# RetNet attention and a SwiGLU FFN on one core: the norm's sums by turned 32x32 blocks on VectorE, and the first turns of q on quarters of TensorE's array

## The chip, the cores and the metric

One core of a Trainium2 chip runs the kernel in one launch. The metric is the device time of an execution in microseconds (us), as the median of several runs. Engines are named as in the profile: PE (TensorE's products), PEld (its weight loads), DVE (VectorE), ACT (ScalarE), POOL (GpSimd), SP (SyncE, which issues most DMAs).

## What is computed

Attention without a softmax, with a decay for each head, and then a gated FFN with an RMS norm in front:

```python
# q, k, v: (8 batches, 8 heads, 576 positions, 64)
scores = scale * np.matmul(q, k.transpose(0, 1, 3, 2))
ret = scores * Dmat            # gamma_h ** (i - j) for i >= j, else 0
x = matmul(ret, v)             # heads side by side: 4608 tokens x 512
rms = np.sqrt(np.mean(x * x, axis=-1, keepdims=True) + 1e-06)
xn = x / rms * rms_g
g = xn @ w_gate                # 512 x 1536
out = (silu(g) * (xn @ w_val)) @ w_out   # 1536 x 512
```

w_gate, w_val and w_out come as float64 and are rounded to float32 on the chip.

## The kernel before, in words

**Attention.** A job is one batch and one pair of heads: 32 jobs, jobs 0 to 7 (batches 0 and 1) in a head of the program and the rest between the later FFN products. A job needs q and k with the head dimension on partitions. For jobs 0 to 7 `turn` makes them on PE with products by the identity: eight products for q (line 236, 64 of the array's columns each), four full transposes for k (line 230), and two transposes for the last 64 positions, the tail (line 245); ACT copies the results out of PSUM in four copies (lines 241 and 252). Later jobs are turned by DVE in `prepare`. `slot(j)` then does the values of job j-1 (`values`, line 379), the scores (line 292) and states (line 315) of job j on PE, the weighing of the scores (line 328) and the running sums of the states (line 341) on DVE, and the carried part of job j-1 (line 399). The scores and values are 64x64 products that use the four quarters of the array in turn; the carried ones of the first jobs use two. DVE writes the result into x (line 425).

**Units.** The 4608 tokens are nine units of 512. x of a unit is kept transposed, as 4 chunks of 128 channels x 512 tokens, so the norm's mean runs over partitions. Squares are ACT's (`square`), their sums over chunks DVE's (`gather`, lines 467 and 473).

**The norm.** For units 0 and 1, `norm_1` (line 481) takes the mean with eight products of one column, POOL raises it to -1/2, ACT writes it on the diagonal of four 128x128 blocks (`diagonals`, line 495), and a product of ones with these (line 546, called rb) broadcasts it to all partitions. For units 2 to 8, `root_1` sums over partitions and broadcasts at once with a product of ones with the squares, 128x512 (line 504), and finds the inverse root on full 128x512 tiles, by ACT (lines 506, 509, 516) and DVE (510, 513, 517), `root_2` going on with lines 526 and 529. `scale_x` (line 548) then scales x in four operations, and `sums_of_x` (line 563) forms the sums that the FFN's block products need.

**FFN.** Units 0 and 1 use `up_plain` (line 704, written U in the plan: U002 is unit 0, set 0, product 2) while the weights are still being rounded; units 2 to 8 use `up` (line 644), seven block products in each of six steps, and `across` (line 814) for the second matrix. The rounding of the weights runs in 36 halves, each of three ACT operations (line 1075), three DVE operations for the mantissa (1094, 1098, 1102) and a join (1119); a join lets its set's products start.

**Order.** All instructions are issued in program order on each engine, under a manual schedule. The first part is written out by hand in `PLAN`, one token a task: T turn, V scaling of v, S slot, C the close of the last job, Q a square, G a gather, N and D and X the norm's steps (R, Y and X for unit 2), w a step of the rounding, a an ACT step of it, A half a product of `across`. The later units run in a loop: in the last step of `up(u, 5)` the gathers and `root_1` of the next unit stand between its seven products, and `root_2`, `scale_x` and `sums_of_x` between those of `across(u)`. The loads are issued in the order of `LOADS`, the tails of q, k and v in `load_tails` (line 190), on ACT's queue for job 0 and on SP's for the others. PSUM has eight banks in one pool.

Of the kernel before, what the change touches and what calls it, by code (L numbers as in the profile page):

```python
# [14 lines left out]
P = 128  # L15
L = P // 2
SQ = 32
# [27 lines left out]
def kernel(  # L45
# [59 lines left out]
    mean_w = cell("mean_w", 1.0 / DM)  # L105
    mhalf = cell("mhalf", -0.5)
    eps = cell("eps", EPS)
    most = cell("most", 1151.0 + 7.5 / 16)
    top = cell("top", 255.0 * 2.0**23)
    guess = cell("guess", 0x5F1FFFF9 + 2.0**22 * np.log2(DM))  # L110
# [72 lines left out]
    def load_tails(i, queue):  # L183

        b, heads = TAILS[i]
        for n, (nm, src) in enumerate((("qt", q), ("kt", k), ("vt", v))):
            at = NV + (3 * b + n) * DM
            t = vi[:TAIL, at : at + DM].rearrange("p (h d) -> p h d", d=D)
            cut = slice(heads[0], heads[-1] + 1)
            queue.dma_start(  # L190
                out=t[:, cut], in_=src[b, cut, NFULL * P :].rearrange("h p d -> p h d")
            )
            for hp in range(heads[0] // 2, heads[-1] // 2 + 1):
                st[b * NHP + hp][nm] = t[:, 2 * hp : 2 * hp + 2]
# [27 lines left out]
    def turn(j):  # L222

        d = st[j]
        n = NFULL
        for nm in "qk":
            ps = bank(f"turn_{j}_{nm}")
            for c in range(n):
                if nm == "k":
                    nc.tensor.transpose(  # L230
                        out=ps[:, c * P : c * P + P],
                        in_=d["k"][:, c].rearrange("p e d -> p (e d)"), identity=ident,
                    )
                    continue
                for e in range(2):
                    nc.tensor.matmul(
                        ps[side(e), c : n * P : n], lhsT=d["q"][:, e, c], rhs=ident,
                        start=True, stop=True,
                    )
            t = d[nm + "T"] = att.tile([P, S], F32, tag=nm + "T", name=f"{nm}T_{j}")  # L240
            nc.scalar.copy(out=t[:, : n * P], in_=ps[:, : n * P])
        last = bank(f"turn_{j}_t")
        for i, nm in enumerate("qk"):
            o = slice(i * TAIL, i * TAIL + TAIL)
            nc.tensor.transpose(
                out=last[:, o], in_=d[nm + "t"].rearrange("p e d -> p (e d)"),
                identity=ident[:TAIL, :TAIL],
            )
        warm_up(j == 0, 2 * P)
        for i, nm in enumerate("qk"):  # L250
            o = slice(i * TAIL, i * TAIL + TAIL)
            nc.scalar.copy(out=d[nm + "T"][:, NFULL * P :], in_=last[:, o])
# [211 lines left out]
    def gather(u, c, sq):  # L464

        if c == NHP - 1 and u > 1:
            nc.vector.scalar_tensor_tensor(
                out=sq, in0=t_of[u], scalar=EPS * DM / P, in1=sq, op0=ALU.add, op1=ALU.add
            )
        elif u < 2 and c == NHP - 1:  # L470
            sq = (t_of[u], sq)
        elif c:
            nc.vector.tensor_tensor(out=sq, in0=t_of[u], in1=sq, op=ALU.add)
        t_of[u] = sq

    def norm_1(u):

        ms = bank(f"ms_{u}")
        for s in range(NS):
            for i, sq in enumerate(t_of[u]):  # L480
                nc.tensor.matmul(
                    ms[:, s : s + 1], lhsT=sq[:, s * P : s * P + P], rhs=mean_w,
                    start=(i == 0), stop=(i == 1),
                )
        r = tmp.tile([P, NS], F32, tag="r", name=f"r_{u}", bufs=1)
        nc.scalar.activation(out=r, in_=ms[:, :NS], func=AF.Relu, bias=eps)
        nc.gpsimd.tensor_tensor(out=r, in0=r, in1=mhalf.to_broadcast([P, NS]), op=ALU.pow)
        t_of[u] = r

    def diagonals(u):  # L490

        r = t_of[u]
        t_of[u] = row(f"diag_{u}")
        for s in range(NS):
            nc.scalar.activation(
                out=t_of[u][:, s * P : s * P + P], in_=ident, func=AF.Copy, scale=r[:, s : s + 1]
            )

    def root_1(u):


        y = t_of[u]
        s = bank(f"ms_{u}")
        nc.tensor.matmul(s, lhsT=ones, rhs=y, start=True, stop=True)
        e = row(f"e_{u}")
        nc.scalar.activation(
            out=y.bitcast(U32), in_=s.bitcast(U32), func=AF.Relu, bias=guess, scale=-0.5
        )
        nc.scalar.activation(out=e, in_=y, func=AF.Square)
        nc.vector.scalar_tensor_tensor(  # L510
            out=e, in0=e, scalar=-1.0 / DM, in1=s, op0=ALU.mult, op1=ALU.mult
        )
        nc.vector.scalar_tensor_tensor(
            out=y, in0=e, scalar=K0, in1=y, op0=ALU.add, op1=ALU.mult
        )
        nc.scalar.activation(out=e, in_=y, func=AF.Square)
        nc.vector.scalar_tensor_tensor(
            out=e, in0=e, scalar=K1 * K1 / DM, in1=s, op0=ALU.mult, op1=ALU.mult
        )
        t_of[u] = y, e  # L520

    def root_2(u):


        y, e = t_of[u]
        nc.vector.scalar_tensor_tensor(
            out=e, in0=e, scalar=-10.0 / 3.0, in1=e, op0=ALU.add, op1=ALU.mult
        )
        nc.vector.scalar_tensor_tensor(
            out=y, in0=e, scalar=5.0, in1=y, op0=ALU.add, op1=ALU.mult  # L530
        )
        t_of[u] = y
# [4 lines left out]
    def scale_x(u, chunks):  # L537
# [3 lines left out]
        g = rms_k  # L541
        rb = t_of[u]
        if u < 2:
            g = rms_g
            rb = bank(f"rb_{u}")
            nc.tensor.matmul(rb, lhsT=ones, rhs=t_of[u], start=True, stop=True)
        for c in chunks:
            nc.vector.scalar_tensor_tensor(
                out=x[:, c], in0=x[:, c], scalar=g[:, c : c + 1], in1=rb,
# [601 lines left out]
    def store_blocks(n):  # L1151
# [7 lines left out]
        T0 V0 a1 S0 a1 T1 a1 a1 V1 S1 T2 V2 F8 S2 V3 T3 w1 a1 w1 Q0 a1 a1 G0 Q1 a1 S3 T4 G1 V4  # L1159
        a1 a1 w1 Q2 a1 S4 a1 V5 w1 T5 G2 V6 Q3 a1 a1 G3 a1 S5 w1 T6 V7 w1 Q4 a1 S6 N0 a1 w1 a1  # L1160
        D0 a1 a1 G4 a1 T7 a1 w1 a1 w1 a1 a1 a1 Q5 X0 G5 S7 w1 U000 w1 a1 a1 a1 Q6 a1 C7 G6 a1 Q7
        G7 U001 N1 w1 w1 w1 D1 U002 w1 a1 X1 a1 w1 a1 w1 w1 w1 w1 a1 a1 a1 w1 a1 U003 a1 w1 w1
# [11 lines left out]
        G9 b1 i4 Q10 k0 Q11 a1 b2 A0 i5 A0 a1 a1 G10 A0 j6 A0 A0 A0 a1 P12 A0 j7 b3 A0 j8 c2 A1  # L1174
        c0 F13 A1 v1 A1 c3 A1 j9 o0 G11 A1 A1 j10 A1 A1 j11 A1 i12 A1 R2 A1 Y2 A1 X2 M2 p1 a1 a1
# [54 lines left out]
    def start():  # L1230
# [3 lines left out]
        def table(i, queue):  # L1234
# [25 lines left out]
            "G": lambda j: gather(*squares.pop(0)), "N": norm_1, "D": diagonals, "X": norm_2,  # L1260
# [6 lines left out]
            "r": refill, "W": weights_to, "A": lambda u: next(outs[u], None), "R": root_1,  # L1267
            "Y": root_2, "M": sums_of_x, "o": store, "p": lambda _: later.pop()(),
            "k": lambda _: nc.vector.tensor_scalar(
                out=rms_k, in0=rms_g, scalar1=3.0 / 8.0 * K1, scalar2=None, op0=ALU.mult  # L1270
            ), "U": lambda n: up_plain(n // 100, n // 10 % 10, n % 10),
# [8 lines left out]
    with tc.manual_schedule():  # L1280
        start()
        for u in range(2, NU):
            j0 = NHP * (u + 1)
            more = u + 1 < B
            for n in range(2 * NG):
                for i, _ in enumerate(up(u, n)):
# [9 lines left out]
                    if u + 1 < NU and n == 2 * NG - 1:  # L1296
                        if i < NHP:
                            gather(u + 1, i, square(u + 1, i))
                        elif i == NHP:
                            root_1(u + 1)  # L1300
# [7 lines left out]
            for i, _ in enumerate(across(u)):  # L1308
                if u + 1 == NU:
                    continue  # L1310
                if i == 2:
                    root_2(u + 1)
# [31 lines left out]
```

## Time and profile before

| | us |
|---|---|
| median of 3 runs | 1104.73 (1101.4 to 1110.42) |
| span of the profiled execution | 1104.5 |
| PE busy in the span | 1091.5 |
| DVE busy | 751.7 |
| ACT busy | 339.7 |
| POOL busy | 458.0 |
| first product of up for unit 0 (U000) | 57.38 |
| start of up for unit 2 | 306.02 |

The profile shows one execution of 1104.5 us; its own time is that of the middle run to 0.2 us. A line of a timeline gives the start, the time until the last instruction of the group ended, the engine, the line of the kernel, the operation, the tile written and those read, shapes and the number of instructions; in brackets stands how long the engine had nothing to do before, and what ended that. One float32 product is two instructions (passes) on PE, a float32 transpose one. Ends of PE's instructions are modelled and overlap, so PE's cost is read from start to start.

### The profile page before, as it was taken

The numbers are of one execution on the slowest core, as the hardware profiler recorded it, in microseconds if no ns is written. First come the engines' busy times: TensorE is split into PE (matmuls) and PEld (weight loads), VectorE is DVE, ScalarE is ACT, GpSimd is POOL, SyncE is SP. The second block draws the span as 40 slices with busy tenths as digits, with TensorE's granted clock in tenths as the row PEclk, the third lists the DMA queues.
The fourth block names the chain that finished last, engine by engine and source line by source line (L and its number), as shares of the span: only waits on it lengthen the run. The fifth ranks groups of instructions, "written<-read, shape, count | busy, mean of one in ns | idle before, by whom it ended". The sixth has DMA issues, their size and how long they took to land.

```text
span 1104.5 us, 24454 instructions
## 1 busy us (share of the span) xinstructions
PE 1091.5 (99%) x10102; PEld 915.1 (83%) x10102; DVE 751.7 (68%) x1219; ACT 339.7 (31%) x757; POOL 458.0 (41%) x421
## 2 busy tenths in 40 slices
PE   8899999999999999999999999999999999999998
PEld 7654444479988899889988998889888998898898
DVE  3778568877866794678657775668565935594457
ACT  5855564331124412342034303330233111211110
POOL 0026325538430196027802581239321942393236
PEclk9899999999999999999999999999999999999999
DMA  8847777696978866787678865887475755585461
GB/s 211 197 139 259 280 244 217 208 343 185 289 277 227 216 251 226 185 238 235 253 215 199 285 259 149 245 246 284 143 203 198 273 193 176 183 293 158 152 247 43
DMA packets 253871, 243.60 MB, mean 221 GB/s; under 512 B 193216, under 2 KB 213824, under 8 KB 247616
## 3 DMA queue, kind: packets, MB, share of 16 engines
q1 hardware_dynamic: 252320, 241.64, 69.1%
q8 instruction: 79, 1.29, 0.5%
q10 hardware_dynamic: 1440, 0.40, 0.2%
q14 instruction: 32, 0.26, 0.1%
HBM read 211.92 MB, written 30.08 MB: 219 GB/s over the span
## 4 chain that ended last, share of the span: by engine, by line
PE 96%; DVE 1%; issue 1%; ACT 0%; POOL 0%; POOLq 0%; DVEq 0%; ACTq 0%
PE up L704 15%; PE x L644 14%; PE w L644 13%; PE z L644 13%; PE y L644 7%; PE xo L814 6%; PE xp L814 4%; PE zo L814 4%; PE zp L814 3%; PE wo L814 2%; PE yo L814 2%; PE av L379 2%; PE wp L814 2%; PE av L399 2%; PE s L292 2%; PE yp L814 2%
## 5 line engine op out<-in xcount | busy, mean ns | idle before, releaser
L704 PE MATMUL up<-x,ring 128*128 128x512 f32 x384 | 167.1, 595 | 0.0
L644 PE MATMUL x<-x,ring 128*128 128x256 f32 x672 | 161.1, 383 | 0.0
L644 PE MATMUL w<-sums,ring 128*128 128x256 f32 x672 | 158.9, 379 | 0.0
L644 PE MATMUL z<-x,ring 128*128 128x256 f32 x672 | 158.8, 379 | 0.0
L766 POOL TENSOR_TENSOR vi<-h 128x384 f32<-128x384 f32 x32 | 39.5, 1234 | 275.2 <-DVE h L663 266.3
L704 PEld LDWEIGHTS up<-x,ring 128*128 128x128 f32 x384 | 72.3, 190 | 89.3 <-issue 84.8
L644 PEld LDWEIGHTS z<-x,ring 128*128 128x128 f32 x672 | 127.8, 190 | 19.8 <-issue 2.9
L644 PEld LDWEIGHTS w<-sums,ring 128*128 128x128 f32 x672 | 127.7, 190 | 17.2
L644 PEld LDWEIGHTS x<-x,ring 128*128 128x128 f32 x672 | 125.5, 190 | 17.4 <-ACT m L670 0.2
L771 POOL TENSOR_TENSOR vi<-h 128x384 f32<-128x384 f32 (+2 forms) x46 | 46.4, 1009 | 149.5 <-DVE h L663 149.5
L1010 POOL TENSOR_TENSOR vi<-vi 128x512 f32<-128x512 f32 (+1 forms) x77 | 78.1, 1027 | 37.9 <-DVE vi L841 21.5
L644 PE MATMUL y<-sums,ring 128*128 128x256 f32 x336 | 79.4, 379 | 0.0
L670 ACT COPY m<-x 128x512 f32<-128x512 f32 x42 | 24.6, 586 | 173.4 <-PE x L644 173.4
L651 DVE TENSOR_TENSOR h<-u,w 128x512 f32<-128x512 f32 x42 | 28.9, 688 | 67.8 <-PE w L644 67.8
L651 DVE TENSOR_TENSOR u<-m,y 128x512 f32<-128x512 f32 x42 | 28.8, 687 | 63.4 <-PE y L644 62.7
L644 PEld LDWEIGHTS y<-sums,ring 128*128 128x128 f32 x336 | 63.9, 190 | 8.6
L665 ACT ACTIVATE h<-h 128x512 f32<-128x512 f32 x63 | 39.7, 630 | 84.1 <-DVE h L651 84.1
L1130 POOL TENSOR_TENSOR vi<-vi 128x512 f32<-128x512 f32 (+1 forms) x24 | 40.7, 1696 | 30.8 <-DVE vi L1119 17.3
L651 DVE TENSOR_TENSOR u<-u,z 128x512 f32<-128x512 f32 x42 | 28.9, 688 | 33.7 <-PE z L644 33.6
L1130 POOL TENSOR_TENSOR ring<-ring 128x512 f32<-128x512 f32 x24 | 30.4, 1272 | 49.3 <-DMA w_up_blocks<-ring 44.1
L771 POOL TENSOR_TENSOR vi<-vi,h 128x384 f32<-128x384 f32 (+2 forms) x46 | 47.6, 1034 | 3.6
L771 POOL TENSOR_TENSOR vi<-h,vi 128x384 f32<-128x384 f32 (+2 forms) x46 | 46.9, 1019 | 3.6
(314 smaller groups left out, 2086.5 us busy)
## 6 DMA issues: line engine op xcount, KB each, us to landing
ring<-w_out_blocks SPq DMA_DIRECT2D x59, 1344.0 KB, 6.4
ring<-w_up_blocks SPq DMA_DIRECT2D x42, 1792.0 KB, 7.7
w_out_blocks<-vi SPq DMA_DIRECT2D x21, 448.0 KB, 5.9
out_dram<-vi SPq DMA_DIRECT2D x64, 128.0 KB, 3.0
qraw<-in_q_dram SPq DMA_DIRECT2D x96, 72.0 KB, 5.1
kraw<-in_k_dram SPq DMA_DIRECT2D x96, 72.0 KB, 2.5
k<-in_k_dram SPq DMA_DIRECT2D x48, 128.0 KB, 2.9
v<-in_v_dram SPq DMA_DIRECT2D x48, 128.0 KB, 2.8
```

The source lines that it names most:

```text
L292: nc.tensor.matmul(s[e][side(odd), i * L : i * L + L], lhsT=d["kT"][side(e), c * L : c * L + L], rhs=d["qT"][side(e), c * L : c * L + L], ...
L379: mm = nc.tensor.matmul(av[odd][column(j, odd, e), i * L : i * L + L], lhsT=d["v"][side(odd), i, e] if c < NC - 1 else d["vt"][:, e], rhs= ...
L644: nc.tensor.matmul(ps[:, i * HU : i * HU + HU], lhsT=w[:, PLACE[blk], c, i * P : i * P + P], rhs=t_of[u][blk][:, c], start=(start and i == ...
L651: nc.vector.tensor_tensor(out=o, in0=a, in1=pairs_of(ps), op=ALU.add)
L665: nc.scalar.activation(out=o, in_=c, func=AF.Silu)
L670: nc.scalar.copy(out=s1, in_=pairs_of(x_))
L704: nc.tensor.matmul(ps, lhsT=w[:, PLACE[blk], c % 2, i * P : i * P + P], rhs=x_of[u][:, c], start=(c == 0), stop=(c == NHP - 1),)
L766: eng.tensor_tensor(out=i1, in0=x12, in1=x11, op=ALU.subtract)
L771: eng.tensor_tensor(out=o[:, c], in0=a[:, c], in1=b[:, c], op=op)
L814: nc.tensor.matmul(ps, lhsT=lhs[:, c], rhs=w[:, s, c], start=((nm, s // 4) not in first), stop=False, skip_group_check=True,)
L1010: eng.tensor_tensor(out=t[:, :, o], in0=t[:, :, x], in1=t[:, :, y], op=ALU.add)
L1130: nc.gpsimd.tensor_tensor(out=t[o], in0=t[x], in1=t[y], op=op)
```

## The change

**The turn of jobs 0 to 7.** q is loaded as before, but each of its eight products is cut into two of 64x64, one for each half of the rows; the two halves write to two banks. The tails of q and k are loaded to the two halves of the partitions of one tile, and one full transpose turns both; it is issued ahead of k's four. ACT again makes four copies: q's first 256, its other 320, k's tail, k.

**The norm of all units.** The squares of all four chunks are summed (for units 0 and 1 two were summed and the rest left to the product). `fold` reduces the 128x512 sums over groups of 32 with a transpose inside 32x32 blocks, which gives 128x16; `meet` multiplies that with a 128x128 matrix `alike` that has ones where two partitions agree modulo 32; `root` finds the inverse root with eight DVE operations on 128x16, and a DVE transpose of the result, repeated along the free axis, writes it to all partitions of a PSUM bank as 128x512. `scale_x` reads that bank. `same_rows` makes `alike` from the identity in two DVE operations early in the plan. The factor rms_k, made late before, is now made ahead of X0.

**The plan.** For unit 0, N0 stands after G3 (before S5), R0 before S6, Y0 after it, k0 ahead of X0. For unit 1: N1 after G7, R1 after U001, Y1 two steps before U002. For unit 2: N2 two half products before R2. In the loop the fold takes the place of `root_1`, `meet` is issued after the seventh product, and `root` takes the place of `root_2`.

```diff
     def load_tails(i, queue):
         b, heads = TAILS[i]
-        for n, (nm, src) in enumerate((("qt", q), ("kt", k), ("vt", v))):
-            at = NV + (3 * b + n) * DM
-            t = vi[:TAIL, at : at + DM].rearrange("p (h d) -> p h d", d=D)
-            cut = slice(heads[0], heads[-1] + 1)
+        cut = slice(heads[0], heads[-1] + 1)
+        for n, (nm, src) in enumerate((("q", q), ("k", k), ("vt", v))):
+            at = NV + (2 * b + n // 2) * DM
+            t = vi[:, at : at + DM].rearrange("p (h d) -> p h d", d=D)
+            rows = side(n % 2)
...
     def turn(j):
-        for nm in "qk":
-            ps = bank(f"turn_{j}_{nm}")
...
-                for e in range(2):
-                    nc.tensor.matmul(
-                        ps[side(e), c : n * P : n], lhsT=d["q"][:, e, c], rhs=ident,
-                        start=True, stop=True,
-                    )
...
+        t = [bank(f"turn_{j}_q{r}") for r in range(2)]
+        for c in range(n):
+            for e in range(2):
+                for r in range(2):
+                    nc.tensor.matmul(
+                        t[r][side(e), c : n * L : n], lhsT=d["q"][side(r), e, c],
+                        rhs=ident[side(r), side(r)], start=True, stop=True,
                     )
+        m = n * L
+        nc.tensor.transpose(
+            out=t[1][:, m : m + P], in_=d["qkt"].rearrange("p e d -> p (e d)"), identity=ident
+        )
+        tk = bank(f"turn_{j}_k")
+        for c in range(n):
             nc.tensor.transpose(
-                out=last[:, o], in_=d[nm + "t"].rearrange("p e d -> p (e d)"),
-                identity=ident[:TAIL, :TAIL],
+                out=tk[:, c * P : c * P + P], in_=d["k"][:, c].rearrange("p e d -> p (e d)"),
+                identity=ident,
             )
...
+        nc.scalar.copy(out=qT[:, :m], in_=t[0][:, :m])
+        nc.scalar.copy(out=qT[:, m:], in_=t[1][:, : m + TAIL])
+        nc.scalar.copy(out=kT[:, n * P :], in_=t[1][:, m + TAIL : m + 2 * TAIL])
+        nc.scalar.copy(out=kT[:, : n * P], in_=tk)
...
     def gather(u, c, sq):
-        if c == NHP - 1 and u > 1:
+        if c == NHP - 1:
...
-        elif u < 2 and c == NHP - 1:
-            sq = (t_of[u], sq)
...
-    def norm_1(u):
...
-    def diagonals(u):
...
-    def root_1(u):
...
-    def root_2(u):
...
+    def fold(u):
+        t = column_of(f"fold_{u}")
+        nc.vector.tensor_reduce(
+            out=t, in_=t_of[u].rearrange("p (b j) -> p b j", j=SQ), axis=mybir.AxisListType.X,
+            op=ALU.add, apply_transpose=True,
+        )
+        t_of[u] = t
...
+    def meet(u):
+        t = t_of[u]
+        s = t_of[u] = bank(f"ms_{u}")[:, :NB]
+        nc.tensor.matmul(s, lhsT=alike, rhs=t, start=True, stop=True)
...
+    def root(u):
+        s = t_of[u]
+        y, e = column_of(f"y_{u}"), column_of(f"e_{u}")
+        def step(o, a, c, b, op0, op1=ALU.mult):
+            nc.vector.scalar_tensor_tensor(out=o, in0=a, scalar=c, in1=b, op0=op0, op1=op1)
+        nc.vector.tensor_scalar(
+            out=y.bitcast(U32), in0=s.bitcast(U32), scalar1=-0.5, scalar2=GUESS,
+            op0=ALU.mult, op1=ALU.add,
         )
+        nc.vector.tensor_tensor(out=e, in0=y, in1=y, op=ALU.mult)
+        step(e, e, -1.0 / DM, s, ALU.mult)
+        step(y, e, K0, y, ALU.add)
+        nc.vector.tensor_tensor(out=e, in0=y, in1=y, op=ALU.mult)
+        step(e, e, K1 * K1 / DM, s, ALU.mult)
+        step(e, e, -10.0 / 3.0, e, ALU.add)
+        step(y, e, 5.0, y, ALU.add)
+        t_of[u] = bank(f"rows_{u}")
+        nc.vector.transpose(
+            out=t_of[u].rearrange("p (b j) -> p b j", j=SQ),
+            in_=y.unsqueeze(2).to_broadcast([P, NB, SQ]),
+        )
...
     def scale_x(u, chunks):
...
-        if u < 2:
-            g = rms_g
-            rb = bank(f"rb_{u}")
-            nc.tensor.matmul(rb, lhsT=ones, rhs=t_of[u], start=True, stop=True)
...
     PLAN = """
-        T0 V0 a1 S0 a1 T1 a1 a1 V1 S1 T2 V2 F8 S2 V3 T3 w1 a1 w1 Q0 a1 a1 G0 Q1 a1 S3 T4 G1 V4
-        a1 a1 w1 Q2 a1 S4 a1 V5 w1 T5 G2 V6 Q3 a1 a1 G3 a1 S5 w1 T6 V7 w1 Q4 a1 S6 N0 a1 w1 a1
-        D0 a1 a1 G4 a1 T7 a1 w1 a1 w1 a1 a1 a1 Q5 X0 G5 S7 w1 U000 w1 a1 a1 a1 Q6 a1 C7 G6 a1 Q7
-        G7 U001 N1 w1 w1 w1 D1 U002 w1 a1 X1 a1 w1 a1 w1 w1 w1 w1 a1 a1 a1 w1 a1 U003 a1 w1 w1
+        T0 V0 a1 S0 K0 a1 T1 a1 a1 V1 S1 T2 V2 F8 S2 V3 T3 w1 a1 w1 Q0 a1 a1 G0 Q1 a1 S3 T4 G1 V4
+        a1 a1 w1 Q2 a1 S4 a1 V5 w1 T5 G2 V6 Q3 a1 a1 G3 N0 a1 S5 w1 T6 V7 w1 Q4 a1 R0 S6 Y0 a1 w1 a1
+        a1 a1 G4 a1 T7 a1 w1 a1 w1 a1 a1 a1 Q5 k0 X0 G5 S7 w1 U000 w1 a1 a1 a1 Q6 a1 C7 G6 a1 Q7
+        G7 N1 U001 R1 w1 w1 Y1 w1 U002 w1 a1 X1 a1 w1 a1 w1 w1 w1 w1 a1 a1 a1 w1 a1 U003 a1 w1 w1
...
                         elif i == NHP:
-                            root_1(u + 1)
+                            fold(u + 1)
+                        elif i == 6:
+                            meet(u + 1)
...
                 if i == 2:
-                    root_2(u + 1)
+                    root(u + 1)
```

## The prediction

> **What bounds the kernel now.** I read the page first, then the busy time by stage, then the timelines of the two places that the change touches. The page's first part puts TensorE (PE) at 99% of the span. The busy time by stage says where that figure can be trusted (columns: stretch, its length, then busy time with instructions of PE, PEld, DVE, ACT, POOL; granted clock; DMA share; GB/s).
>
> ```profile
> PE 1091.5 (99%) x10102; PEld 915.1 (83%) x10102; DVE 751.7 (68%) x1219; ACT 339.7 (31%) x757; POOL 458.0 (41%) x421
> ```
>
> ```profile
> 29.68:50.90 21.22, 18.49 (x515) 16.04 (x513) 19.94 (x53) 16.96 (x45) 1.29 (x4) 0.96 0.88 212
> 50.90:73.00 22.10, 21.83 (x257) 12.96 (x256) 13.09 (x30) 10.23 (x22) 4.18 (x6) 0.89 0.44 123
> 73.00:306.00 233.00, 232.27 (x1510) 143.60 (x1510) 178.45 (x300) 97.65 (x191) 114.77 (x95) 1.00 0.76 251
> 306.00:1093.00 787.00, 786.14 (x7161) 714.76 (x7160) 522.25 (x778) 197.42 (x455) 333.58 (x301) 1.00 0.68 217
> ```
>
> There are two regimes. From 73 us on PE is busy for 1018.4 of 1020 us at clock 1.00: what leaves its queue there leaves the span. In the head it isn't so: from 29.68 to 50.90 VectorE (DVE) is busy for 19.94 of 21.22 us and PE for 18.49. The head holds all eight turns and the norms of units 0 and 1; the steady part holds seven norms.
>
> One norm of the steady part on PE:
>
> ```profile
> 503.79 1.02 PE L504 MATMUL ms<-sq,ones 128*128 128x512 f32 x2
> 504.64 1.89 PE L644 MATMUL z<-x,ring 128*128 128x256 f32 x8
> ```
>
> PE loses 504.64 - 503.79 = 0.85 us to it, with no wait ahead. In the head, first PE, then DVE:
>
> ```profile
> 8.25 0.81 PE L292 MATMUL s<-qT,kT 64*64 64x64 f32 x40
> 8.88 0.28 PE L315 MATMUL s<-h 64*64 64x64 f32 x2
> ...
> 23.27 1.09 PE L236 MATMUL turn_q<-ident,h 128*64 128x128 f32 x16
> 24.30 0.65 PE L230 MATMUL turn_k<-ident,h 128*128 128x128 f32 x4
> 24.89 0.34 PE L245 MATMUL turn_t<-ident,vi 64*128 64x64 f32 x2
> ...
> 45.37 1.95 PE L481 MATMUL ms<-mean_w,sq 128*128 128x1 f32 x16
> 47.24 0.87 PE L236 MATMUL turn_q<-ident,ring 128*64 128x128 f32 x11
> 49.43 0.80 PE L236 MATMUL turn_q<-ident,ring 128*64 128x128 f32 x5 [1.32 <-issue]
> ...
> 51.61 2.08 PE L546 MATMUL rb<-diag,ones 128*128 128x512 f32 x2
> ...
> 57.38 3.70 PE L704 MATMUL up<-x,ring 128*128 128x512 f32 x8
> ```
>
> ```profile
> 29.68 0.48 DVE L341 SCALAR_TENSOR_TENSOR sum<-sum,gc,last 128x256 f32<-128x256 f32 x1 [2.19 <-ACT sum L349]
> ...
> 53.72 2.72 DVE L548 SCALAR_TENSOR_TENSOR x<-x,rms_g,rb 128x512 f32<-128x512 f32 x4 [2.83 <-PE rb L546]
> ...
> 63.28 0.95 DVE L425 TENSOR_TENSOR x<-av,gq 128x256 f32<-128x256 f32 x4 [2.29 <-PE av L399]
> ...
> 72.98 2.72 DVE L548 SCALAR_TENSOR_TENSOR x<-x,rms_g,rb 128x512 f32<-128x512 f32 x4 [3.65 <-PE rb L546]
> ```
>
> The reader is to see DVE's idle brackets: between 29.68 and the scaling of unit 0 it really waits once, 2.83 us for the broadcast rb, and that wait is what the change removes while it puts work of its own in the same place.
>
> **The change, part by part: the seven norms of units 2 to 8.** PE drops the 128x512 product with ones, 0.85 us, and gets meet, two passes of 16 columns. Small full-array products cost (47.24 - 45.37)/16 = 0.117 us a pass in the row of L481, so meet is 0.23 us. From below, two passes at the 0.016 us of the score row are 0.03; from above, half the wide product, 0.43. I take 0.23, the nearest in shape: 7 x 0.62 = **4.3 us off the path**, ends 2.9 and 5.7. Does meet wait? It needs fold, and fold's DVE queue is free at 505.49, after the multiplication into h that begins at 504.71 and takes 0.78. PE reaches meet after products z and w, moved up to 503.79 (1.73 each, from 504.64 to the next row's 506.37): 507.25. Fold has 1.76 us; the dense 128x512 row of DVE is 0.69. For unit 2 fold stands behind work that ends at 290.80 and meet comes at 293.11. No wait. Behind meet, PE's next unit needs x; today the sums of x end at 532.3 and PE wants them at 540.9, so 8.6 us cover root. There DVE drops five wide operations (0.69 + 1.17 + 0.69 + 1.21 + 1.37 = 5.1 us) for fold, eight narrow ones and a transpose, 3.3 us by the rows below. ScalarE's three operations a norm and GpSimd's power go too; PE waits for neither, so nothing is counted.
>
> **The head, DVE.** New in unit 0 ahead of the scaling: the third sum (0.69), a wait for ScalarE's square 3 (it ends at 39.69, DVE is free at about 39.1: 0.6), fold (0.69), root, and 0.2 for rms_k. Root is eight dependent 128x16 operations and a transpose. The row of dependent 128x64 operations of L341 has 285 ns, its 128x192 ones 413, so 1.0 ns an element: 285 - 48 = 0.24 us each, 1.9 in all; bounds 1.3 (the 128x64 product of L425, 216 ns, less 48) and 2.5 (0.31 start to start). [...] The transpose: 736 to 771 ns for 576 elements, 0.70 for 512. So root 2.6, and all of it 4.8 us. DVE ended its queue at 50.89, so X0 starts at 50.89 + 4.8 = 55.7, against 53.72. What PE does earlier doesn't move this: DVE is full from 29.68, and that start hangs on ScalarE, busy without a gap from 24.47, after only 0.34 us of idle time. same_rows lies in DVE's 2.6 us of idle time before 14.90.
>
> **The head, PE.** A turn's q: 16 passes in 24.30 - 23.27 = 1.03 us become 32 on quarters in the order of the scores, whose row has 40 in 8.88 - 8.25 = 0.63 us: 0.50. Tails: two products, 25.15 (the next row) - 24.89 = 0.26 us, become one like a quarter of k's 0.59: 0.15. That is 0.64 us a turn, 5.1 for eight; the norms of 0 and 1 free 1.87 + 2.0 + 1.70 + 0.86 - 2 x 0.23 = 6.0. All 11 us are PE time, and DVE takes the cover away. Both tail loads keep their number, queue and place, but the tail product now stands ahead of k's: job 1's tail came at 13.26, so k's 0.59 and its copy start behind that wait, some 0.85 us later, which the faster turns of jobs 2 and 3 pay back. The four ScalarE copies of a turn stay four, 0.1 us longer. For the PSUM bank that rows_0 holds from Y0 to X0 I count nothing: if turn 7 had to wait for one, PE stands there anyway, and the price is nothing until the 6 us below are used up.
>
> PE comes to U000 some 6 us early and stands until x's first chunk, 55.7 + 0.74 = 56.4, against 57.38. A standing PE has a price here:
>
> ```profile
> 48.00:49.00 1.00, 0.11 (x3) 0.00 (x0) 0.99 (x4) 0.97 (x3) 0.72 (x1) 1.00 0.54 82
> 49.00:50.00 1.00, 0.57 (x5) 0.40 (x4) 0.96 (x2) 1.00 (x4) 0.00 (x0) 0.57 0.55 90
> 50.00:51.00 1.00, 1.00 (x7) 0.71 (x4) 0.85 (x2) 0.73 (x2) 0.00 (x0) 0.50 0.82 134
> ```
>
> After 1.4 us of standing the granted clock is 0.50 until 56, and rb takes 2.0 us for 0.86. The same over U000 would add 0 to 3.5 us to its 3.6. [...] From U000's end (60.0 to 63.5; today 61.0) values and carried of job 7 follow (2.1), then on DVE x (0.95), two sums (1.3), fold (0.7), and the three mantissa operations and the join that U002 needs (2.5): 62.1 + 5.5 = 67.6 or, late, 71. DVE's own sum says no earlier than 68.5: X0's end 58.4, then 0.6 + 0.8 + 1.7 + 0.9 + 0.6 of job 7's work, 63.0, and the same 5.5. U002 started at 68.40 today and U003 at 72.78; now U002 starts at 68.5 to 71 and U003 3.5 later, 72.0 to 74.5. X1 (root and one step later, 73 to 75) meets U100 in time. That is a gain of 0.8 or a loss of 1.7, by the clock; **I take 0**. The ends add root's bounds, 0.6 us in each of two units: a gain of 2.0 and a loss of 2.9.
>
> **Sum.** The profiled execution spans 1104.5, 0.2 below the median 1104.73, so what lies around it is 0.2. 1104.5 - 4.3 - 0 + 0.2 = **1100.4**, 0.4% less; with the ends, 1104.7 - 5.7 - 2.0 = 1097.0 to 1104.7 - 2.9 + 2.9 = 1104.7.
>
> **Rivals.** (1) The head pays in full: DVE isn't what holds U000, or its new operations are short. Against it: 19.94 busy of 21.22. For it: PE is itself at 18.49 and much waits crosswise. 1104.7 - 4.3 - 11.0 = 1089.4; half of it, 1095. (2) Slower: no row shows a reduction with a transpose. If it ran at a quarter of the dense rate, fold is 2.8 us: each head norm loses 2.1 and each of units 3 to 8 has PE waiting 1.0 at meet, 4.2 + 6.0 - 4.3 = 5.9, so 1110.6; at an eighth (5.5 us), 1132. It decides from fold = 2.05 us (2 x 1.36 + 6 x 0.29 = 4.4). For it: the shape is new; against it: the 32x32 transposes run at the dense rate. (3) The quarters do not overlap, as in the row of L399 (32 passes in about 1.05 us): the turns gain nothing, but the head is DVE's; 1100.4 again, at most 1101.
>
> **How the numbers follow.** The forecast with (3) has 0.77, (1) 0.13, (2) 0.10. About 1% (11 us) is what a measurement of this kernel can tell from no change: its runs lie from 1101.4 to 1110.4. Faster by more needs less than 1093.7: nearly all of (1), 0.12. Slower by more needs over 1115.8: fold beyond 3.4 us, 0.05. Within: 0.83. The range takes the forecast's ends and the half of (1), 1095, on one side, the near half of (2) on the other: 1094 to 1107.
>
> **What would show it.** Right: meet without idle time before it, about 0.25 us between its neighbours' starts; fold near 0.7 us; idle PE before U000 with DVE as releaser and a clock under 1.00; X0 near 55.7; U003 within 2 us of 72.8. Wrong: U000 before 54 (the head pays), or PE waiting on fold at meet (the slower case).

## The result, and the profile after

The changed kernel takes 1112.72 us (median of 9 runs, 1109.64 to 1116.55), the kernel before 1105.25 beside it (9 runs, 1101.4 to 1110.42): ratio 1.0063, 95% interval 1.0048 to 1.0079. It is 7 us slower, where 4.3 us less were forecast. The profiled execution took 1113.29, with a span of 1111.5 for 1104.5.

The page's first part, and the busy time by stage over the same stretches as before (columns as there):

```profile
PE 1080.1 (97%) x10190; PEld 908.2 (82%) x10190; DVE 737.5 (66%) x1275; ACT 322.9 (29%) x726; POOL 441.4 (40%) x419
```

```profile
29.68:50.90 21.22, 14.12 (x561) 12.98 (x562) 16.30 (x42) 14.58 (x40) 0.27 (x3) 0.96 0.82 205
50.90:73.00 22.10, 19.38 (x299) 12.03 (x297) 19.69 (x54) 10.04 (x19) 1.55 (x4) 0.88 0.43 112
73.00:306.00 233.00, 224.68 (x1414) 133.76 (x1415) 176.88 (x296) 96.87 (x189) 112.16 (x92) 0.99 0.75 237
306.00:1093.00 787.00, 786.50 (x7198) 717.93 (x7198) 499.61 (x817) 185.85 (x437) 317.08 (x299) 1.00 0.71 222
```

Every engine has less to do, and the span is longer. PE's busy time fell by 11.4 us. The prediction had reckoned with 15.4 (4.3 and 11); on the pages the up products of the FFN alone take 4.0 us of it back (171.1 us in all for 167.1), since some of them ran at a lower clock (0.50 from 59.60 to 62.90, U000 below among them, and from 80.10 to 86.80). The gaps between PE's instructions grew by 18 us. The last row is as full as before, so the loss is ahead of it. The first row holds what the forecast ruled out: DVE, full there before with 19.94 us, has 16.30, and PE 14.12. Both wait.

The steady part did what it should. PE around meet, in the norm of the same unit as before, and the fold ahead of it on DVE:

```profile
514.79 1.89 PE L637 MATMUL w<-sums,ring 128*128 128x256 f32 x8
516.51 0.29 PE L505 MATMUL ms<-fold,alike 128*128 128x16 f32 x2
516.65 1.58 PE L807 MATMUL xo<-ring,h 128*128 128x128 f32 x12
```

```profile
514.68 0.70 DVE L483 TRANSPOSE_TENSOR_REDUCE fold<-sq 128x16 f32<-128x512 f32 x1
```

From meet's start to its neighbour's it is 0.14 us for 0.85, with no wait. From the start of up for unit 2 to the end, 798.48 us became 794.29 (1104.5 - 306.02 and 1111.5 - 317.21): 4.2 less for six norms. That start itself moved from 306.02 to 317.21, and there the loss is. PE at the end of the head:

```profile
49.33 0.69 PE L295 MATMUL s<-qT,kT 64*64 64x64 f32 x14 [3.46 <-issue]
...
58.67 0.33 PE L402 MATMUL av<-qT,sum 64*64 64x64 f32 x3 [1.40 <-issue]
...
59.68 5.29 PE L697 MATMUL up<-x,ring 128*128 128x512 f32 x8 [0.68 <-DVE x L541]
...
67.05 3.70 PE L697 MATMUL up<-x,ring 128*128 128x512 f32 x8
...
72.87 1.98 PE L697 MATMUL up<-x,ring 128*128 128x512 f32 x4 [0.18 <-DVE ring L1112]
82.45 27.75 PE L697 MATMUL up<-x,ring 128*128 128x512 f32 x59 [7.59 <-DVE x L541]
```

U000 starts at 59.68 (57.38 before), and its eight passes take 5.29 us for 3.70. The row at 82.45 begins with U003, which stands 7.59 us and is released by L541, the scaling. U003 belongs to unit 0, whose x has been ready since 61.5. The DVE rows beside it:

```profile
58.78 2.72 DVE L541 SCALAR_TENSOR_TENSOR x<-x,rms_k,rows 128x512 f32<-128x512 f32 x4
...
72.74 0.17 DVE L515 TENSOR_SCALAR y<-ms 128x16 uint32<-128x16 uint32 x1
72.94 1.25 DVE L519 TENSOR_TENSOR e<-y 128x16 f32<-128x16 f32 x1
74.23 0.17 DVE L513 SCALAR_TENSOR_TENSOR e<-e,ms 128x16 f32<-128x16 f32 x1
74.43 1.10 DVE L513 SCALAR_TENSOR_TENSOR y<-e,y 128x16 f32<-128x16 f32 x1
...
79.68 2.71 DVE L541 SCALAR_TENSOR_TENSOR x<-x,rms_k,rows 128x512 f32<-128x512 f32 x4
```

X0 is at 58.78, X1 at 79.68 (53.72 and 72.98 before). X1's last reading of rows_1 ends at 82.39, and U003 starts 0.06 us later: it has waited for a unit that it doesn't read.

Last, PE's waits from 0 to 90 us that the profile puts down to "issue" (PE stood idle, and waited for nothing that the profile shows): before, then after (columns: what waited, for what, us in all, times, longest). An idle time of PE is called a stand below.

```profile
PE turn_q L236 <- issue: 2.3, 2, 1.3
...
PE av L399 <- issue: 0.8, 1, 0.8
...
PE s L292 <- issue: 0.4, 1, 0.4
```

```profile
PE av L402 <- issue: 4.3, 3, 1.8
PE s L295 <- issue: 3.5, 1, 3.5
...
PE s L318 <- issue: 1.5, 1, 1.5
PE turn_q L235 <- issue: 1.3, 1, 1.3
...
PE av L382 <- issue: 0.7, 1, 0.7
```

3.5 us became 11.3. (The texts below count 4.8 and 12.2: the same sums over the whole span.)

### The profile page after: what moved, and what is told of

Read it like the earlier page. It is cut to its first block, busy times and chain, and to the rows that moved or that the text cites. A ratio compares the mean times of both kernels' runs of the same rounds, so it can differ in the third digit from the quotient of the medians.

```text
span 1111.5 us, 24657 instructions
## 1 busy us (share of the span) xinstructions
PE 1080.1 (97%) x10190; PEld 908.2 (82%) x10190; DVE 737.5 (66%) x1275; ACT 322.9 (29%) x726; POOL 441.4 (40%) x419
## 4 chain that ended last, share of the span: by engine, by line
PE 94%; DVE 3%; issue 1%; DMA 1%; SPq 0%; ACT 0%; POOL 0%; POOLq 0%; DVEq 0%; ACTq 0%
PE up L697 15%; PE x L637 13%; PE w L637 13%; PE z L637 13%; PE y L637 7%; PE xo L807 6%; PE xp L807 4%; PE zo L807 4%; PE zp L807 3%; PE wo L807 2%; PE yo L807 2%; PE av L382 2%; PE s L295 2%; PE wp L807 2%; PE av L402 2%; PE yp L807 2%
## 5 line engine op out<-in xcount | busy, mean ns | idle before, releaser
L697 PE MATMUL up<-x,ring 128*128 128x512 f32 x384 | 171.1, 605 | 8.4 <-DVE x L541 8.3
L759 POOL TENSOR_TENSOR vi<-h 128x384 f32<-128x384 f32 x32 | 42.8, 1338 | 274.5 <-DVE h L656 264.8
L764 POOL TENSOR_TENSOR vi<-h 128x384 f32<-128x384 f32 (+2 forms) x46 | 43.8, 953 | 150.2 <-DVE h L656 150.2
L426 ACT COPY x<-av 128x192 f32<-128x192 f32 (+6 forms) x136 | 37.8, 278 | 29.5 <-PE av L402 28.0
L764 POOL TENSOR_TENSOR vi<-h,vi 128x384 f32<-128x384 f32 (+2 forms) x46 | 44.6, 969 | 3.6
```

The lines of the kernel that those rows point to most:

```text
L426: nc.scalar.copy(out=o, in_=part)
L697: nc.tensor.matmul(ps, lhsT=w[:, PLACE[blk], c % 2, i * P : i * P + P], rhs=x_of[u][:, c], start=(c == 0), stop=(c == NHP - 1),)
L759: eng.tensor_tensor(out=i1, in0=x12, in1=x11, op=ALU.subtract)
L764: eng.tensor_tensor(out=o[:, c], in0=a[:, c], in1=b[:, c], op=op)
```

## The experiments

Four theories. **1, the bank:** the eight PSUM banks are handed out in turn, and rows_1, which lies in one from root to the end of the scaling, holds U003's. **2, the quarters:** the turn in twice as many PE instructions makes PE stand for issue. **3, the tail** ahead of k's four products holds the turns of the first jobs. **4, VectorE's work:** the head's norms put fold and root on a DVE that is already full. All ratios are to the kernel before on the same chip, with 95% intervals; a difference of two ratios is turned into us with 1105.5.

### The parts by themselves

**Rows in SBUF.** In the changed kernel:

```diff
-        t_of[u] = bank(f"rows_{u}")
+        t_of[u] = temp(f"rows_{u}") if u < 2 else bank(f"rows_{u}")
```

> The changed kernel, but for units 0 and 1 root writes its row of factors into SBUF and not into a PSUM bank. Theory 1 (bank): the eight banks go round in order, and the eighth request after rows_1 is the bank of U003, so U003 stands 7.59 us until X1 has read rows_1 for the last time (82.39; U003 at 82.45). Without it U003 follows U002 at about 74.9, U100 is then held by X1's first chunk (about 80.4), and of the 7.6 us and the half clock behind them (5.3 us for eight passes in place of 3.6) some 6 to 8 come back: 1105 to 1107. Theory 2 (the quarters: PE's idle time put down to issue, 12.2 us in the changed kernel's head against 4.8): the same lateness shows up at the next product, and no more than 2 us come back: 1111 to 1113. Theory 3 (the tail product ahead of k's four): no change, 1112 to 1113.

Measured: 1108.15 us, ratio 1.0029 (1.0015 to 1.0043), 3.8 us less than the changed kernel's ratio gives. PE from U002's second half on:

```profile
76.12 1.98 PE L697 MATMUL up<-x,ring 128*128 128x512 f32 x4 [0.18 <-DVE ring L1112]
78.80 3.70 PE L697 MATMUL up<-x,ring 128*128 128x512 f32 x8 [0.69 <-ACT h L705]
83.82 3.67 PE L697 MATMUL up<-x,ring 128*128 128x512 f32 x8 [1.33 <-DVE x L541]
89.06 6.25 PE L697 MATMUL up<-x,ring 128*128 128x512 f32 x14 [1.56 <-DVE ring L1112]
```

U003 (78.80) follows U002 and no longer waits for X1; 7.59 us of standing became 0.69 + 1.33 + 1.56 = 3.58. The profile names no banks: that U003 lay in that of rows_1 is shown by its wait for X1's last reading and by this test. Less came back than the 6 to 8 us expected, since U100 (83.82) and U110 (89.06) now stand for X1 and for their weights. The edit moves unit 0's row too, so what came back is the price of both rows.

**The norm alone**, with the old turn and loads:

```diff
-        t = [bank(f"turn_{j}_q{r}") for r in range(2)]
...
+        for nm in "qk":
+            ps = bank(f"turn_{j}_{nm}")
```

> The changed kernel with the old turn and the old loads of tails: the new norm alone. It asks for as many PSUM banks in the same order, so theory 1 (bank) keeps U003 behind X1: 1109 to 1113, with U003 at the end of X1. Theory 2 (the quarters) says that the head's loss goes away with the turn, and the steady part's 4.9 us stay: 1100 to 1104, idle time by issue back near 5 us. Theory 3 (tail product first) says 1 to 3 us less than the changed kernel: 1110 to 1112.

Measured: 1110.45, ratio 1.0048 (1.0032 to 1.0064), issue back at 4.3 us, and U003 again stands 7.59 us for X1. As theory 1 said; theory 2 alone is out.

**The turn alone**, on the kernel before:

```diff
-        for nm in "qk":
-            ps = bank(f"turn_{j}_{nm}")
...
+        t = [bank(f"turn_{j}_q{r}") for r in range(2)]
```

> The kernel before with the turn on quarters and the new loads of tails, and the old norm. Theory 1 (bank): no row of factors is held in PSUM from root to scaling, so the head loses nothing by it; VectorE bounds the head and the turn gains nothing: 1103 to 1106. Theory 2 (the quarters): it loses most of the changed kernel's 11.2 us in the head: 1110 to 1116, with some 12 us of idle time by issue. Theory 3: 1106 to 1108.

Measured: 1111.81, ratio 1.0062 (1.0045 to 1.0079). So theory 1 alone is out too: the turn by itself loses 6.9 us, and U003 doesn't stand in it. Its waits for issue, from 0 to 90 us, sum to 9.6:

```profile
PE s L295 <- issue: 3.1, 1, 3.1
PE turn_q L235 <- issue: 2.1, 1, 2.1
PE s L318 <- issue: 1.8, 1, 1.8
PE av L402 <- issue: 1.8, 1, 1.8
...
PE av L382 <- issue: 0.8, 1, 0.8
```

After the longest, 3.08 us up to 49.55, the clock is at half (0.50 from 50 to 60). Busy time and clock of that stretch (the eighth column is the clock; before: 0.66):

```profile
48.00:58.00 10.00, 8.45 (x130) 8.21 (x131) 4.01 (x12) 2.08 (x6) 1.02 (x1) 0.54 0.77 153
```

**The steady part alone:** the new norm in units 2 to 8 only, on the kernel before.

```diff
+            "n": fold, "R": meet, "Y": root, "K": same_rows,
...
-                            root_1(u + 1)
+                            fold(u + 1)
```

> The kernel before with the new norm in units 2 to 8 alone; units 0 and 1, the turn and the tails as before. All theories put the loss into the head, so here the steady part's 4.9 us stand by themselves: 1100 to 1101, a ratio of 0.9955 to the kernel before. If it comes out above 1103, the loss isn't in the head.

Measured: 1101.34 (1098.42 to 1102.64), ratio 0.9960 (0.9945 to 0.9974): 4.4 us less. This is the fastest version measured, and the forecast's one real gain by itself.

### What issue is

The trace's DMA records have a queue of kind instruction (q8 on the page), with 79 packets of 16 KB before and 80 after. 10102 passes of PE and as many weight loads in 79 packets make 256 PE instructions each. In each of the 17 traces of this study the number of packets is that of PE's instructions divided by 256 and rounded up (78 to 81). In these traces there are 63 stands for issue longer than 0.6 us in the first 90 us, and every one ends 2.2 to 3.3 us after such a packet's transfer began. In the dense stretch of the changed kernel the packets begin 4.1 to 4.5 us apart (18.3, 22.8, 27.0, 31.5, 35.9, 40.0). So PE, as far as can be inferred, has run out of program. The longest of these stands takes 4.0 us (e_pad2 below). The agreement of stands and packets is no proof that the count of instructions decides the time, so it was varied.

**Padding the old turn**, 256 PE instructions more in the head:

```diff
+        for e in range(8):
+            nc.tensor.matmul(
+                last[side(e % 2), 2 * TAIL : 2 * TAIL + 1], lhsT=d["k"][side(e % 2), 0, 0],
+                rhs=d["k"][side(e % 2), 0, 0, :1], start=True, stop=True,
+            )
```

> The kernel before, with the old turn and eight idle quarter products of one column behind the tails of each turn (16 passes with their weight loads, some 0.26 us a turn, no result used): as many PE instructions as the turn on quarters has, 256 more in the head. Theory 2 in its sharper form (PE's instructions come in 16 KB pieces of 256, each about 2.2 to 3.0 us after its request, and every idle time put down to issue ends so): 2 to 6 us more than the kernel before, 1107 to 1111, and idle time by issue over 7 us. Rival (the quarters themselves disturb the array, or the copies of a turn in their new order): 1104.5 to 1107.

Measured: 1109.89, ratio 1.0030 (1.0017 to 1.0043), 3.3 us more; issue 6.1 us, less than the 7 expected. But the idle products take longer than the 0.26 us a turn that was reckoned: in job 2 they begin at 18.49 and the values behind them at 18.87, so 0.38 us, or 3.0 us for eight turns. Their own time can make up the whole loss, and this run doesn't decide for theory 2.

**Twice the padding:**

```diff
-        for e in range(8):
+        for e in range(16):
```

> As e_pad with sixteen idle quarter products behind the tails of each turn: 512 PE instructions more in the head than before, two pieces of 16 KB. Theory 2 (instructions): twice e_pad's loss of 3.3 us or more, 1111 to 1115. Rival (e_pad's loss was a shift of where the pieces fall): 1106 to 1110.

Measured: 1117.82, ratio 1.0122 (1.0090 to 1.0155): 13.5 us more, four times the loss for twice the padding. The sixteen products of a turn take 0.84 us from their start to that of the values behind them, 6.7 us for eight turns:

```profile
36.83 1.03 PE L250 MATMUL turn_t<-ring 64*64 64x1 f32 x29
37.67 0.27 PE L384 MATMUL av<-ret,h 64*64 64x64 f32 x1
```

So some 7 us are left. Issue sums to 6.9 us, 3.4 more than before, and one stand alone is 4.0:

```profile
PE av L404 <- issue: 4.4, 2, 4.0
PE turn_q L236 <- issue: 2.5, 2, 1.5
```

Here the padding costs more than its own time, but what the rest consists of wasn't separated. Padding adds work as well as instructions; the next run takes instructions away and leaves PE's time nearly as it is.

**The other direction:** the turn on quarters with 256 instructions taken away (it adds 240). Half of carried's products of the first eight jobs (the second head) are left out, and that part of x is not computed.

```diff
-            for e in range(2):
+            for e in range(1 if j < FIRST else 2):
                 mm = nc.tensor.matmul(
                     av[odd][column(j, odd, e), i * L : i * L + L], lhsT=d["sum"][side(e), c - 1],
```

> The turn on quarters alone, and in the first eight jobs the products of carried for the second head left out: eight products, 16 passes and 16 weight loads a job, so that the head has as many PE instructions as before the change. (That part of x is then not computed.) Theory 2 (instructions): idle time by issue back to 5 us or less, and most of the turn's loss gone: 1104 to 1107. Rival (the quarters or the order of the copies cost, whatever the count of instructions): some 2 us less for the shorter carried, 1109 to 1111.

Measured: 1105.39, ratio 1.0004 (0.9986 to 1.0023). 6.4 us of the turn's 6.9 are gone, and issue falls from 9.6 to 5.9:

```profile
PE turn_q L235 <- issue: 2.8, 2, 1.8
...
PE av L402 <- issue: 1.1, 1, 1.1
PE last L318 <- issue: 0.8, 1, 0.8
...
PE av L382 <- issue: 0.6, 1, 0.6
PE s L295 <- issue: 0.6, 1, 0.6
```

PE's work hardly got shorter: from the start of carried to that of the turn's tail product (line 240) PE takes 1.54 us in the turn alone and 1.49 with half of carried's products left out. In the turn alone, then here:

```profile
42.76 1.08 PE L402 MATMUL av<-qT,sum 64*64 64x64 f32 x30
...
44.30 0.33 PE L240 MATMUL turn_q<-ident,vi 128*128 128x128 f32 x1
```

```profile
35.24 1.03 PE L402 MATMUL av<-qT,sum 64*64 64x64 f32 x15
...
36.73 0.33 PE L240 MATMUL turn_q<-ident,vi 128*128 128x128 f32 x1
```

This is the test that decides for theory 2: fewer instructions for nearly the same work, and the loss is gone.

**Its control**, the same products left out of the kernel before (that part of x is not computed there either):

```diff
-            for e in range(2):
+            for e in range(1 if j < FIRST else 2):
```

> The control of e_less_turn: the kernel before with the same products of carried left out (that part of x is not computed), 256 instructions fewer in the head than it had. Theory 2 (instructions): idle time by issue under 3.5 us, 1 to 4 us less than the kernel before: 1102 to 1105. Rival: less by the shorter carried alone, at most 2 us, 1104 to 1106; then e_less_turn stands 5 us or more above it.

Measured: 1106.51, ratio 1.0010 (0.9994 to 1.0027). That is above both ranges. Issue fell to about 1.5 us, but nothing was gained: PE now stood 1.5 us for ACT's copy of kT and 0.7 us for a transfer of q, which it hadn't before. So the shorter carried isn't what brought e_less_turn back, and instructions taken away below the old count gained nothing.

**Whole products for q**, which need q in k's layout:

```diff
-            st[j]["q"] = room.rearrange("p (e t d) -> p e t d", e=2, d=D)
...
+                nc.tensor.transpose(
+                    out=ps[:, c * P : c * P + P], in_=d[nm][:, c].rearrange("p e d -> p (e d)"),
+                    identity=ident,
+                )
```

> The kernel before, with q loaded in the layout of k and turned like k in four products over the whole array, one pass each: 12 passes and 12 weight loads fewer in each turn, 192 instructions fewer in the head, and 0.4 us of PE time less a turn. q's transfers come in pieces of 256 bytes for 1 KB. Theory 2 (instructions): idle time by issue under 4 us and 1 to 4 us less than the kernel before, 1101 to 1104.5, unless the smaller pieces hold back the first jobs. Rival (VectorE alone sets the head): 1104.5 to 1107.

Measured: 1110.30, ratio 1.0044 (1.0026 to 1.0061). Issue fell to 1.6 us as theory 2 said, but the smaller pieces of q's transfers held back v and q (up to 90 us PE waits 8.2 us for ACT, 5.6 of them for the scaled v, and 3.3 for DMAs). As a test of the time it is inconclusive.

**The tail behind k's four**, on the turn alone:

```diff
-        nc.tensor.transpose(
-            out=t[1][:, m : m + P], in_=d["qkt"].rearrange("p e d -> p (e d)"), identity=ident
-        )
         tk = bank(f"turn_{j}_k")
...
+        nc.tensor.transpose(
+            out=t[1][:, m : m + P], in_=d["qkt"].rearrange("p e d -> p (e d)"), identity=ident
+        )
         warm_up(j == 0, 2 * P)
```

> The turn on quarters alone with the one tail product moved behind k's four: the wait for the tail's transfer (1.31 and 2.30 us ahead of jobs 0 and 1) no longer holds k. Theory 3 (tail product first): 1 to 3 us less than with the tail ahead (1111.81), 1108.5 to 1111. Theory 2 (instructions): no change beyond 1 us, 1111 to 1113, since PE makes up for the wait and stands for its code later.

Measured: 1113.76, ratio 1.0059 (1.0038 to 1.0080), against 1.0062: no change. Theory 3 falls.

These seven runs show one thing more. Six had a mean granted clock of 0.991 or 0.992 and took 1112.48 to 1115.20 us; one had 1.000 and took 1105.75, as the kernel before. The traces agree: in the turn alone the clock is 0.85 over the first 70 us, for 0.93 before and 0.93 in e_less_turn. Up to 90 us PE's waits sum to 15.9 us for 7.1 before, 8.8 more, and U000 comes 7.1 us later (64.45 for 57.38), though the turns were to be 5.1 us shorter; that leaves some 3.4 us for slower products. So part of the turn's loss is paid at a lower clock, and not in the stands themselves. Whether the stands bring the lower clock about wasn't tested.

### What is left of the norm in the head

**The norm alone, rows in SBUF**, with the old turn and loads as in e_norm_only:

```diff
-        t_of[u] = bank(f"rows_{u}")
+        t_of[u] = temp(f"rows_{u}") if u < 2 else bank(f"rows_{u}")
```

> The new norm with the old turn, and the rows of units 0 and 1 in SBUF: what the held bank costs where the turn plays no part. With the rows in PSUM this kernel took 1110.45, and PE stood 7.59 us for X1 ahead of U003. Theory 1 (bank) says 4 to 7 us less, 1104 to 1107, with U003 right behind U002 and a shorter stand before U100. Its rival (VectorE's longer work makes X1 late whatever bank it is, and U100 pays what U003 paid): 1109 to 1111.

Measured: 1106.65, ratio 1.0007 (0.9996 to 1.0019). The bank costs 0.0041, 4.5 us. Against the steady part alone, 5.2 us are still missing.

**Root of units 0 and 1 by a power on GpSimd:**

```diff
+        if u < 2:
+            nc.scalar.activation(out=y, in_=s, func=AF.Relu, scale=1.0 / DM)
+            nc.gpsimd.tensor_tensor(out=y, in0=y, in1=mhalf.to_broadcast([P, NB]), op=ALU.pow)
```

> As e_norm_rows (the new norm, the old turn, rows of units 0 and 1 in SBUF), but in units 0 and 1 the eight narrow VectorE operations of root give way to one copy on ScalarE and one power of 128x16 on GpSimd, whose queue is nearly empty there. Theory 4 (what is left of the head's loss, 1106.65 against 1101.34 with the old norm in units 0 and 1, is VectorE's added work: it is busy 26.4 of the 30 us from 60 to 90, and root of unit 1 took 4.4 us there): the 1.6 and 4.4 us come off VectorE, X1 starts 3 to 4 us sooner, and the time is 1102.5 to 1105. Rival (the rest is the order in which PE is fed, not VectorE's length): 1106 to 1108.

Measured: 1106.77, ratio 1.0009 (0.9992 to 1.0027), no gain. DVE shows why:

```profile
75.53 0.71 DVE L512 STREAM_TRANSPOSE rows<-y 128x512 f32<-128x512 f32 x1 [6.93 <-POOL y L510]
```

GpSimd was at the sums of weight set 0 until 72.6, and the power itself took 2.9 us there. X1 came at 78.06, later than the 76.86 of e_norm_rows. The test exchanged DVE's work for a wait and doesn't decide theory 4. (The 26.4 us in the text above are those of e_rows_sbuf; e_norm_rows has 29.09, and the kernel before 22.48.)

**One unit at a time:** the new norm in units 2 to 8 and in unit 0, or in unit 1 (rows in SBUF), the old one in the other. Theory 5 is that the rest of the loss is unit 1's alone. The edit for unit 0 (for unit 1 the last figure is 0):

```diff
-        if c == NHP - 1 and u > 1:
+        if c == NHP - 1 and u != 1:
```

> The old turn; the new norm in units 2 to 8 and in unit 0 (rows in SBUF), the old one in unit 1. Theory 5 (what is left of the loss is unit 1's: its fold and root queue on a full VectorE, so X1 comes at 76.9 for 73.0 and PE stands for it ahead of U100): as with the old norm in both, 1099 to 1102.5, or less, since unit 0's 3.5 us of PE products go. Rival (unit 0's, by a later X0): 1104 to 1106.5.

> The mirror of e_norm0: the new norm in unit 1 and in 2 to 8, the old one in unit 0. Theory 5 (unit 1's): 1104 to 1107, with stands of PE ahead of U100 and U110 of some 3 us in all. Rival (unit 0's): 1100 to 1102.5.

Measured: unit 0 1103.20, ratio 0.9981 (0.9967 to 0.9995); unit 1 1104.39, ratio 0.9987 (0.9972 to 1.0003). Against 0.9960 that is 2.3 and 3.0 us, together 5.3, near the 5.2. Each of the two is only just clear of its interval, some 2.2 us either way. As far as they go, both units share the loss, and not unit 1 alone as theory 5 had it. Unit 1's price can be read on PE:

```profile
67.23 1.98 PE L727 MATMUL up<-x,ring 128*128 128x512 f32 x4 [0.20 <-DVE ring L1142]
69.90 3.70 PE L727 MATMUL up<-x,ring 128*128 128x512 f32 x8 [0.69 <-ACT h L735]
74.93 3.67 PE L727 MATMUL up<-x,ring 128*128 128x512 f32 x8 [1.33 <-DVE x L571]
80.07 10.14 PE L727 MATMUL up<-x,ring 128*128 128x512 f32 x23 [1.47 <-DVE ring L1142]
```

3.5 us ahead of U003, U100 and U110, where the kernel before has no gap. Unit 0's shows on DVE alone: with the new norm X0 starts at 56.56, with the old one at 53.72 (before) and 51.32 (e_steady). These two have nearly the same head and differ by 2.4 us, so single traces don't give unit 0's price. X0 in the run with unit 0 new:

```profile
56.56 2.74 DVE L571 SCALAR_TENSOR_TENSOR x<-x,rms_k,rows 128x512 f32<-128x512 f32 x4
```

**The scaling of unit 1 moved up:**

```diff
-        G7 N1 U001 R1 w1 w1 Y1 w1 U002 w1 a1 X1 a1 w1
+        G7 N1 U001 R1 w1 w1 Y1 X1 w1 U002 w1 a1 a1 w1
```

> As e_norm_rows, with the scaling of unit 1 moved up right behind its root, ahead of the mantissa step that it stood behind (X1 at about 75.0 for 76.9). Theory 5: PE's stand of 1.33 us ahead of U100 goes and the one for the weights of U110 stays or grows: 0.5 to 1.5 us less than e_norm_rows (1106.65), 1105 to 1106.3. Rival: no change, since the weights' steps come later by what X1 gains.

Measured: 1107.97, ratio 1.0022 (1.0009 to 1.0036), 1.7 us more than e_norm_rows. The weights pay, and by more than the rival said:

```profile
81.12 9.45 PE L694 MATMUL up<-x,ring 128*128 128x512 f32 x15 [3.46 <-DVE sums L1092]
```

DVE is nearly full here (29.09 of the 30 us from 60 to 90 in e_norm_rows, 25.5 to 26.4 in the changed kernel, e_rows_sbuf and e_norm_only, 22.48 before), and an order seems only to choose which product waits.

### The sum

In us against the kernel before: steady part -4.4; the norm of units 0 and 1 on DVE +5.2; the bank +4.5; the turn on top of that 1.0063 - 1.0048 = +1.7. Together +7.0, by construction, since each is the difference of neighbouring runs. Each carries an interval of some 1.6 to 2.5 us either way, so the turn's +1.7 isn't clear of nothing; the other three are.

## Why the prediction was wrong, step by step

- **Steady part, 4.3 us:** right; 4.4 by itself, 4.2 for six norms in the trace. The cause is as forecast. meet is 0.14 us for the 0.23 taken, fold 0.70 for 0.69, and nothing waits at meet: rival (2) falls with its threshold of 2.05 us.
- **Root on DVE:** 0.24 us an operation was taken; it is 0.17 busy and 0.205 from start to start, and 2.3 us with the transpose for 2.6. The eight take 1.65 where GpSimd rests, for the 1.9 reckoned. In unit 1 they took 4.4, some 2.8 more: three of the eight operations took 0.92 to 1.25 us, all while GpSimd ran its sums of weight set 0. The trace has three additions there, ending at 74.16, 75.50 and 76.87; each slow operation began inside one and ended 0.03 to 0.04 us after its end, while those that read ms in PSUM took 0.17 inside them. No step counted that.
- **X0 at 55.7:** 55.64 to 56.77 in the four kernels with the old turn and this root in unit 0, so the working was right as far as DVE goes. In the changed kernel it was 58.78: "what PE does earlier doesn't move this" failed. PE was not earlier but later; DVE stood for it (16.30 us busy of 21.22).
- **"All 11 us are PE time, and DVE takes the cover away":** the PE time did go, and the quarters overlap (32 passes in about 0.6 us, so rival (3) falls). The step left out the idle time by issue, 3.5 us in rows that the profile of before had, and that more instructions in less time make it longer. Alone the turn loses 6.9 us, part of it at a lower clock.
- **The clock at U000, 0 to 3.5 us:** inside the bounds. U000's eight passes took 5.29 us for 3.70, so 1.6 more. The term stood for U000 alone; all up products together took 4.0 us more.
- **"For the PSUM bank that rows_0 holds from Y0 to X0 I count nothing":** the reason was given for rows_0 and turn 7. The bank on which PE stood is rows_1's. With both rows in SBUF 4.5 us come back.
- **"X1 (root and one step later, 73 to 75) meets U100 in time":** 79.68 in the changed kernel, 74.0 at best (e_norm1), with U100 standing 1.33 us. The bounds, 0.8 gained to 1.7 lost, held DVE's sum to U002 but not what stands on DVE between U002 and U110.
- **The tail ahead of k:** PE stood 2.55 us for job 1's tail, and as forecast the wait is paid back: putting it last changes nothing.

What failed is thus the step "I take 0", the head's share of the sum: in the traces the head lost 11.9 us by the start of up for unit 2 (11.2, and 0.7 of unit 2's own gain), and by the medians 11.4 (7.0 and 4.4). Rival (1), the head that pays in full, had the wrong sign. A head that loses by a held bank, by a longer norm on DVE and by PE's program was not on the list: the bank was mentioned and priced at nothing, the norm was bounded at 0.6 us a unit, and the program stood in the profile as "issue".

Open: why the turn costs 6.9 us beside the old norm, and 1.7 (or 2.4 with the rows in SBUF: 1.0029 - 1.0007) beside the new one. The new norm frees PE instructions in the head, and its kernels wait on DVE there anyway; neither was separated. How the 6.9 divide between the stands and the lower clock is open too, and so is the path from X0's 3 to 5 us to unit 0's 2.3. That the 5.2 us of the head's norms are DVE's work is argued from its busy time and from the stands ahead of U003, U100 and U110; the one test that took work off DVE put a wait in its place.

## What to carry to other kernels

Where a stage's idle time is put down to issue, and its products are small and dense, count PE's instructions: doubling their number for half the time each lost 6.9 us here by itself, where 5.1 were to be saved. Before a result is left in PSUM until a later task, count the requests to the pool from there on: the product that got the same bank here (U003) stood 7.59 us for that task, whose result it does not read. And an engine with free time in the mean is no place for new work in the one stage where it is full (DVE here: 68% of the span, 94% from 29.68 to 50.90); the same change was worth 4.4 us when it was kept out of the head.

## What the hardware showed that was not expected

- As far as the packets show, PE's program came in 16 KB pieces of 256 instructions (79 for 20204 before, 80 for 20380 after); at the 63 stands it is 2.2 to 3.3 us from a piece's start to PE's going on. With 256 instructions fewer for nearly the same work the turn's loss fell from 6.9 us to 0.4.
- A narrow DVE operation (128x16) that takes 0.17 us took 0.92 to 1.25 us beside GpSimd's 128x512 additions, the same three of eight in the changed kernel and in e_norm_rows. Each ended 0.03 to 0.04 us after the addition in which it began.
- A power of 128x16 on GpSimd took 2.9 us, where its 128x4 form took 1.0 in the kernel before.
- A reduction with a transpose inside 32x32 blocks ran at the rate of a dense addition: 0.70 us for 128x512, where the addition of L470 took 0.69.
